# One sink matmul for each pair of heads, and an earlier fetch of the first weight tiles, in a fused attention and MLP kernel

## The chip, the cores and the metric

The kernel runs on one core of a Trainium2 chip. Its engines work side by side, each through a queue of its own, in order: PE (TensorE: matmuls, and transpositions made as matmuls), DVE (VectorE), ACT (ScalarE), POOL (GpSimd) and SP (SyncE, which here only issues DMAs). They wait for one another through semaphores. The metric is the device time of one execution in microseconds, the median of several runs.

## The reference

Attention with sinks and a sliding window, then a two-layer MLP, in float32:

```python
batch, n_heads, seq, head_dim = (4, 8, 768, 64)
n_sink, window = (4, 128)
n_tokens, d_model, d_ff = (3072, 512, 2048)
...
scores = scale * np.matmul(q, k.transpose(0, 1, 3, 2))
is_sink = pos[None, :] < int(n_sink)
in_window = (rel >= 0) & (rel < int(window))
scores = np.where(is_sink | in_window, scores, -1000000000.0)
a = np.exp(scores - np.max(scores, axis=-1, keepdims=True))
a = a / (np.sum(a, axis=-1, keepdims=True) + 1e-09)
x = np.matmul(a, v)        # heads side by side: (3072, 512)
...
h = x @ w_in
out = np.maximum(0.01 * h, h) @ w_out
```

## The kernel before

**Units, heads, steps.** The work is cut into eight units `u`: a batch and one half of its 768 rows, three blocks of 128 rows each (`T = 3`, `TU = 384` columns). A unit has eight heads in four pairs. The attention of a unit is a stream of 60 steps (`attention_stream`), its MLP a stream of 112 steps (`mlp_stream`, 16 slices `fc` of the hidden width). Units 0 and 1 (`u < EARLY`) take the plain path, units 2 to 7 a path with split operands. PE's order is written out by hand: the loop at the end of `fast_path` first draws 70 attention steps alone (`att_steps + LEAD0`), then weaves both streams, about two MLP steps for each attention step, so that the MLP of unit `u` runs beside the attention of the units after it. The other engines' orders are made by a scheduler from the program.

**Split operands.** From unit 2 on, and in the MLP always, a float32 operand is taken as a sum of two parts, hi (rounded by a cast) and lo (the rest, a subtraction), and a product is made of three: hi x hi, hi x lo, lo x hi. For weights the cast is on ScalarE (L179) and the subtraction on GpSimd (L180); for queries and keys L235, L236, L238; for values L249 and L250.

**A head.** Each of three row blocks `j` has its scores (L270, a bank of PSUM of its own, `s`, one buffer), a mask (L298), the row maximum (L306, which frees the bank), the exponential (L309) and the division (L310, L311, L315). `tail` turns a block round on PE (L355), copies hi on ScalarE (L362) and lo on VectorE (L363), and GpSimd places both in `pt` (L324). The sums over the keys of the window are `values` (L411).

**Sinks.** The four sink columns of both heads of a pair are gathered in `sk`, transposed once for the pair (L376), and multiplied with a mask `diag` into `sn` (L380), with 16 or 24 rows: row block, head, sink. From unit 2 on they are split: ScalarE copies hi to rows 0 on of a tile `st` (L386), VectorE subtracts lo into rows 32 on (L387, `SKL = 32`). `values` of a head is a group of six or eight matmuls over hi and lo of `pt` and one more of `st` against the sinks' values `ssp` (L409), 256 or 384 columns wide. A head's matmuls give two products in two halves of a bank `v` (one buffer): ScalarE copies one half (L422), VectorE adds the other (L423), into half of the pair's tile `xf`. `emit_x` then casts it (L483) and subtracts (L484), which gives the MLP's operand.

**Banks for transpositions.** `slot()` hands out the banks for transpositions by a running number `n`. In phase 0 they alternate with the MLP's bank `h`, in phase 1 (the MLP of unit 0) there is one bank `t`, and in phase 2 (from the MLP of unit 1 on) odd numbers have a bank `d` and even ones `t`.

**The MLP.** A slice has twelve matmuls into `h` (L530, one buffer), then ScalarE scales (L537), VectorE takes the maximum (L538, which frees `h`), ScalarE casts (L539) and VectorE subtracts (L540, on GpSimd in unit 0). Nine matmuls (L551) into three banks `o` follow a slice later.

**Weights.** There are 32 tiles of 512 KB. `load_weights` fetches one over SP, decodes it in three VectorE instructions (L171, L173, L175), and splits it. The first four (input and output tile of slices 0 and 1) are called for in the 70 attention steps, at steps 20, 32, 44 and 56. `pace` (L166) holds a fetch until an instruction is done: the decode of the tile four before it (`DEPTH`), or, where there are not four yet, the newest softmax maximum, `anchor[0]`. In units 2 to 5 the MLP's stream also fetches each tile again to check the weights' range (`check_weights`: L191 on ScalarE, L193 on GpSimd, L195 on VectorE).

Of the kernel before, what the change touches and what calls it, by code (L numbers as in the profile page):

```python
# [9 lines left out]
F32 = mybir.dt.float32  # L10
F32R = mybir.dt.float32r
# [3 lines left out]
ALU = mybir.AluOpType  # L15
# [5 lines left out]
P = 128  # L21
B, H, S, D = 4, 8, 768, 64
# [16 lines left out]
NVB = (3, 4)  # L39
# [73 lines left out]
def fast_path(ctx, tc, cpool, qk, vu, vs, w_in, w_out, out, ident, wz, lim, masks, tri, diag, negm, wmin, wmax):  # L113
    nc = tc.nc
# [32 lines left out]
    anchor = [None]  # L147
# [5 lines left out]
        return nc.sync.dma_start(out=raw.rearrange("p f t -> p (f t)"), in_=w_out[fc * P:(fc + 1) * P, :])  # L153

    decoded = []

    def pace(dma, after):
        tc.add_manual_dep(dma.ins, after.ins.name,
                          mybir.DependencyInfo(mybir.DependencyClass.Sync, mybir.DependencyReason.SCHED_ONLY),
                          reason="pace")  # L160

    def load_weights():
        fc, nm = len(wts) // 2, "io"[len(wts) % 2]
        raw = wpool.tile([P, 512, 2], I32, tag=f"w{nm}{fc}", name=f"w{nm}raw{fc}")
        dma = fetch(raw, nm, fc)
        pace(dma, decoded[-DEPTH] if len(decoded) >= DEPTH else anchor[0])  # L166
        top, low = raw[:, :, 1], raw[:, :, 0]
        word = ps_t.tile([P, 512], I32, tag="d", name=f"d{nm}{fc}")
        w = iopool.tile([P, 512], F32, tag="io", name=f"w{nm}f{fc}")
        with tc.issue_after(anchor[0].ins):  # L170
            nc.vector.tensor_scalar(out=word, in0=top, scalar1=3, scalar2=0x3FFFFFFF,  # L171
                                    op0=ALU.logical_shift_left, op1=ALU.bitwise_and)
        nc.vector.scalar_tensor_tensor(out=word, in0=top, scalar=-0x40000000, in1=word,  # L173
                                       op0=ALU.bitwise_and, op1=ALU.bitwise_or)
        decoded.append(nc.vector.scalar_tensor_tensor(out=w.bitcast(I32), in0=low, scalar=29, in1=word,  # L175
                                                      op0=ALU.logical_shift_right, op1=ALU.bitwise_or))
        both = wpool.tile([P, 2, 512], F32R, tag=f"w{nm}{fc}", name=f"w{nm}{fc}")
        hi, lo = both[:, 0, :], both[:, 1, :]
        nc.scalar.copy(out=hi, in_=w)  # L179
        nc.gpsimd.tensor_tensor(out=lo, in0=w, in1=hi.bitcast(F32), op=ALU.subtract)  # L180
        wts[nm, fc] = (hi, lo)
# [60 lines left out]
    def split_values(u, h):  # L242
        vr, sr = vraws.pop((u, h))
        vsp = apool.tile([P, 4, 2 * P], F32R, tag="vsp", name=f"vsp{u}_{h}", bufs=1)
        ssp = apool.tile([SKR, 1, 2 * P], F32R, tag="ssp", name=f"ssp{u}_{h}", bufs=1)
        for dst, src, m in ((vsp, vr, NVB[u % 2]), (ssp, sr, 1)):
            sview = src[:, 0:m * P].rearrange("p (n q c) -> p n q c", q=2, c=D)
            hview = dst.rearrange("p n (q c) -> p n q c", c=D)[:, 0:m, 0::3, :]
            nc.scalar.copy(out=hview, in_=sview)  # L249
            nc.gpsimd.tensor_tensor(out=dst[:, 0:m, D:3 * D].rearrange("p n (q c) -> p n q c", c=D),  # L250
                                    in0=sview, in1=hview.bitcast(F32), op=ALU.subtract)
        return vsp, ssp

    raws = {}
# [116 lines left out]
    def sinks(u, pair, sk):  # L371
        half = u % 2
        nj = T - 1 + half
        rows = nj * 2 * NSK
        tp = slot()
        nc.tensor.transpose(out=tp[0:rows, 0:P], in_=sk[:, 0:nj].rearrange("p j h s -> p (j h s)"),  # L376
                            identity=ident)
        sn = xpool.tile([SROWS, T, P], F32, tag="xf", name=f"sn{u}_{pair}")
        sv = sn[0:rows, 0:nj, :]
        nc.vector.tensor_tensor(out=sv, in0=tp[0:rows, 0:P].rearrange("p (o q) -> p o q", o=1).broadcast_to([rows, nj, P]),  # L380
                                in1=diag[0:rows, 0:nj, :], op=ALU.mult)
        sv = sv.rearrange("p j q -> p (j q)")
        if u < EARLY:
            return sv
        st = sts[half]
        nc.scalar.copy(out=st[0:rows, :], in_=sv)  # L386
        nc.vector.tensor_tensor(out=st[SKL:SKL + rows, :], in0=sv, in1=st[0:rows, :].bitcast(F32),  # L387
                                op=ALU.subtract)
        return st

    def values(u, h, pt, st, state):
        half = u % 2
        pair, odd = divmod(h, 2)
        q0 = 0 if half else P
        hp = slice(odd * D, (odd + 1) * D)
        lp = slice((1 - odd) * D, (2 - odd) * D)
        vv, sv = state["v"]
        if u < EARLY:
            if not odd:
                state["acc"] = ps_v.tile([P, 512], F32, tag="v", name=f"v{u}_{h}")  # L400
            out = state["acc"][hp, :]
            mms = [(vv[:, kb * P + odd * D:kb * P + (odd + 1) * D], pt[:, 0, po:po + m], qo, m)
                   for kb, (po, qo, m) in enumerate(segments(half))]
        else:
            out = ps_v.tile([P, 512], F32, tag="v", name=f"v{u}_{h}")
            cs = slice(odd * P, (odd + 1) * P)
            mms = [(vv[:, kb, cs], pt[:, c, po:po + m], qo, m)
                   for kb, (po, qo, m) in enumerate(segments(half)) for c in range(2)]
            mms.append((sv[:, 0, cs], st, q0, TU - q0))  # L409
        for c, (l, r, o, m) in enumerate(mms):  # L410
            nc.tensor.matmul(out[:, o:o + m], lhsT=l, rhs=r, start=c == 0, stop=c == len(mms) - 1,  # L411
                             skip_group_check=True)
        if u < EARLY:
            if odd:
                nc.tensor.matmul(state["acc"][:, q0:TU], lhsT=sv[0:st.shape[0], :], rhs=st, start=False, stop=True,  # L415
                                 skip_group_check=True)
            x = state["acc"][:, 0:TU]
        else:
            if not odd:
                state["xf"] = xpool.tile([P, TU], F32, tag="xf", name=f"xf{u}_{pair}")  # L420
            x = state["xf"]
            nc.scalar.copy(out=x[hp, :], in_=out[lp, 0:TU])  # L422
            nc.vector.tensor_tensor(out=x[hp, :], in0=out[hp, 0:TU], in1=x[hp, :], op=ALU.add)  # L423
        if odd:
            emit_x(u, pair, x)

# [326 lines left out]
def layout(q, k, v, n_sink, window, moe_w_in, moe_w_out):  # L753
    import numpy as np
    c = np.ascontiguousarray
# [13 lines left out]
    s4 = v[:, :, 0:NSK].reshape(B, NPAIR, 2, NSK, D)  # L769
    for r in range(0, SROWS, 2 * NSK):  # L770
        for x in range(2):
            vs[:, :, 0:2, r + x * NSK:r + (x + 1) * NSK, x] = s4[:, :, None, x]
    vs = vs.reshape(B, NPAIR, SKR, P)
    return [("qk0", c(qk0)), ("qk1", c(qk1)), ("vu0", c(vu0)), ("vu1", c(vu1)), ("vs", c(vs)),
            ("qT", c(qt)), ("kT", c(kt)), ("v", c(v)), ("lims", np.stack([n_sink, window])),
# [17 lines left out]
```

## Time and profile before

| | |
|---|---|
| median of 3 runs | 731.52 us (731.45 to 731.6) |
| the profiled execution | 733.14 us |
| its span (first to last instruction) | 731.3 us |
| mean granted clock of PE | 0.993 |
| sink matmuls of units 2 to 7 (L411, `st` and `ssp`) | 48: 24 of 256 columns, 24 of 384 |
| L386 on ScalarE, L387 on VectorE | 24 each, median 460 and 482 ns |
| DMA | 77.77 MB, mean 106 GB/s |
| first MLP matmul | 51.05 us from the span's start |
| first MLP matmul of unit 1 | 149.56 us |

A row of the timeline gives the start, the length, the engine, the source line, the operation, the tile written and the tiles read, the shape, how many in a row, and in square brackets the idle time before it and what ended it. PE's matmuls overlap, so that the distance from one start to the next says more of a matmul's price than its recorded length. Unless said otherwise, times are from the span's start.

### The profile page before, as it was taken

Reading aid. Unit: us, or ns where it says so; the run is one execution under the profiler, and the core shown is the slowest. Engines: PE = TensorE matmul, PEld = TensorE weight load, DVE = VectorE, ACT = ScalarE, POOL = GpSimd, SP = SyncE. Lnnn points to the kernel's source line nnn. Section 1 sums busy time; section 2 is a strip of 40 time slices with the busy share of each in tenths; the row PEclk is TensorE's granted clock in tenths of the full one; section 3 lists DMA queues with packets and bytes.
Section 4 is the critical chain, followed back from the end, with each engine's and each line's share of the span. In section 5 each row is a group of like instructions: output and inputs, shape, how many; then the busy total and the mean of one; then the engine's idle time right before and its main releaser. Section 6 shows DMA issues by size and latency. Waiting matters only on the chain.

```text
span 731.3 us, 12474 instructions
## 1 busy us (share of the span) xinstructions
PE 709.2 (97%) x3871; PEld 619.9 (85%) x3871; DVE 547.3 (75%) x1749; ACT 422.2 (58%) x1178; POOL 370.5 (51%) x500
## 2 busy tenths in 40 slices
PE   8889999999999999999999999999999999999996
PEld 5457887888999889999988989999888999899995
DVE  6778988666667888888888898888888977733222
ACT  5566766667666666656666566666656565522221
POOL 2115657745456677747566676756666555300000
PEclk9999999999999999999999999999999999999999
DMA  5767766221222533234334333324342211001001
GB/s 174 242 211 216 222 193 218 67 95 38 63 70 69 174 116 108 73 130 145 96 98 127 131 106 112 117 88 148 106 127 81 96 62 41 0 1 44 1 0 49
DMA packets 43755, 77.77 MB, mean 106 GB/s; under 512 B 3616, under 2 KB 26400, under 8 KB 43680
## 3 DMA queue, kind: packets, MB, share of 16 engines
q1 hardware_dynamic: 43536, 76.76, 33.1%
q8 instruction: 33, 0.54, 0.3%
q14 instruction: 42, 0.34, 0.1%
q10 hardware_dynamic: 144, 0.13, 0.1%
HBM read 70.58 MB, written 6.29 MB: 105 GB/s over the span
## 4 chain that ended last, share of the span: by engine, by line
PE 83%; DVE 8%; DMA 4%; ACT 3%; issue 1%; SPq 0%; ACTq 0%; DVEq 0%
PE h L530 33%; PE o L551 33%; PE v L411 8%; PE s L270 6%; PE t L355 2%; DVE gl L540 1%; DMA wiraw<-in_w_in 1%; PE warm L575 1%; DMA woraw<-in_w_out 1%; DVE zeroi L195 1%; DVE g L538 1%; DMA coraw<-in_w_out 1%; DMA vsraw<-in_vs 1%; PE v L415 1%; PE t L342 1%
## 5 line engine op out<-in xcount | busy, mean ns | idle before, releaser
L530 PE MATMUL h<-xh,wi 128*128 128x384 f32 x1024 | 314.5, 354 | 1.3 <-DVE g L538 1.3
L551 PE MATMUL o<-wo,gh 128*128 128x512 f32 x768 | 244.4, 399 | 0.0
L530 PEld LDWEIGHTS h<-xh,wi 128*128 128x128 f32 x1024 | 190.5, 188 | 14.2 <-DVE g L538 2.4
L530 PE MATMUL h<-xl,wi 128*128 128x384 f32 x512 | 172.6, 337 | 0.0
L551 PE MATMUL o<-wo,gl 128*128 128x512 f32 x384 | 151.4, 394 | 0.0
L551 PEld LDWEIGHTS o<-wo,gh 128*128 128x128 f32 x768 | 133.8, 188 | 18.1 <-issue 1.8
L324 POOL TENSOR_SCALAR_AFFINE_SELECT pt<-stg 128x256 fp32r<-128x256 f32 x240 | 100.9, 446 | 84.6 <-DVE stg L363 72.0
L538 DVE TENSOR_TENSOR g<-h,g 128x384 f32<-128x384 f32 x128 | 71.0, 555 | 64.0 <-ACT g L537 62.3
L540 DVE TENSOR_TENSOR gl<-g,gh 128x384 fp32r<-128x384 f32 x112 | 92.1, 823 | 16.6 <-ACT gh L539 15.0
L537 ACT ACTIVATE g<-h 128x384 f32<-128x384 f32 x128 | 62.2, 486 | 71.8 <-PE h L530 71.7
L530 PEld LDWEIGHTS h<-xl,wi 128*128 128x128 f32 x512 | 97.0, 189 | 3.3
L236 POOL TENSOR_TENSOR qksp<-qkraw,qksp 64x392 fp32r<-64x392 f32 (+1 forms) x48 | 58.4, 1217 | 62.2 <-issue 45.1
L309 ACT ACTIVATE pk<-pk,negm 128x128 f32<-128x128 f32 (+1 forms) x144 | 58.0, 403 | 50.3 <-DVE negm L306 49.3
L551 PEld LDWEIGHTS o<-wo,gl 128*128 128x128 f32 x384 | 72.2, 188 | 16.9 <-DVE gl L540 0.3
L539 ACT CAST gh<-g 128x384 fp32r<-128x384 f32 x128 | 65.7, 513 | 33.3 <-DVE g L538 30.7
L270 PEld LDWEIGHTS s<-qksp 128*128 128x128 f32 x288 | 53.1, 188 | 7.8 <-issue 1.7
L270 PE MATMUL s<-qksp 128*128 128x260 f32 (+1 forms) x288 | 56.4, 277 | 1.1 <-DVE negm L306 1.1
L238 POOL TENSOR_TENSOR qksp<-qkraw,qksp 128x384 fp32r<-128x384 f32 x48 | 53.9, 1124 | 3.7
L362 ACT CAST stg<-t 128x128 fp32r<-128x128 f32 x120 | 30.8, 257 | 41.6 <-PE t L355 34.7
L411 PEld LDWEIGHTS v<-pt,vsp 128*128 128x128 f32 x336 | 45.1, 189 | 5.8 <-issue 3.3
L315 DVE TENSOR_SCALAR pk<-pk,sm 128x132 f32<-128x132 f32 (+1 forms) x120 | 47.0, 392 | 2.3
L235 ACT CAST qksp<-qkraw 128x776 fp32r<-128x776 f32 (+1 forms) x48 | 42.8, 892 | 8.6 <-PE s L270 8.4
(131 smaller groups left out, 1079.1 us busy)
## 6 DMA issues: line engine op xcount, KB each, us to landing
qkraw<-in_qk SPq DMA_DIRECT2D x27, 454.0 KB, 3.2
qkraw<-in_qk SPq DMA_DIRECT2D x26, 388.0 KB, 3.1
wiraw<-in_w_in SPq DMA_DIRECT2D x16, 512.0 KB, 3.7
woraw<-in_w_out SPq DMA_DIRECT2D x16, 512.0 KB, 4.4
ciraw<-in_w_in SPq DMA_DIRECT2D x16, 512.0 KB, 3.8
coraw<-in_w_out SPq DMA_DIRECT2D x16, 512.0 KB, 3.6
out<-ob SPq DMA_DIRECT2D x23, 256.0 KB, 2.0
vraw<-in_vu SPq DMA_DIRECT2D x14, 256.0 KB, 2.6
```

Source lines behind the costliest of these rows:

```text
L236: nc.gpsimd.tensor_tensor(out=sp[D:P, TU:TU + n], in0=raw[D:P, TU:TU + n], in1=sp[D:P, TU:TU + n].bitcast(F32), op=ALU.subtract)
L238: nc.gpsimd.tensor_tensor(out=sp[:, TU + n:2 * TU + n], in0=raw[:, 0:TU], in1=sp[:, 0:TU].bitcast(F32), op=ALU.subtract)
L270: nc.tensor.matmul(ps[:, 0:kn], lhsT=sp[:, off + j * P:off + (j + 1) * P], rhs=sp[:, TU + k0:TU + k0 + kn], start=c == 0, stop=c == len(pa ...
L309: nc.scalar.activation(out=w, in_=w, func=AF.Exp, scale=-1.0, bias=neg, accum_out=sm)
L324: nc.gpsimd.affine_select(out=out, in_=src, pattern=([[0, x]] if x > 1 else []) + [[sign, P]], base=-1 if prev else 0, channel_multiplier= ...
L411: nc.tensor.matmul(out[:, o:o + m], lhsT=l, rhs=r, start=c == 0, stop=c == len(mms) - 1, skip_group_check=True)
L530: nc.tensor.matmul(ph[:, 0:TU], lhsT=w[:, cs], rhs=x, start=cc == 0 and c == 0, stop=cc == NCC - 1 and c == 2)
L537: nc.scalar.mul(g, ph[:, 0:TU], 0.01)
L538: anchor[0] = nc.vector.tensor_tensor(out=g, in0=ph[:, 0:TU], in1=g, op=ALU.max)
L539: nc.scalar.copy(out=gh, in_=g)
L540: (nc.gpsimd if u == 0 else nc.vector).tensor_tensor(out=gl, in0=g, in1=gh.bitcast(F32), op=ALU.subtract)
L551: nc.tensor.matmul(po[t], lhsT=gg[:, tsl], rhs=w, start=f == 0 and c == 0, stop=f == NFC - 1 and c == 2)
```

## The change

There are two edits.

**Sinks.** The values of the sinks now come from the host in three groups of 32 rows where there were two. `split_values` makes one tile `ssp` of 128 columns: values hi in the first group, lo in the second, hi in the third. `sinks` fills three groups of `st` to match: hi, hi (a second ScalarE cast), lo (the subtraction, now on GpSimd). One matmul for the pair gives all three products for both heads, since the rows of the other head hold zeros in the value columns. It goes into a bank from `slot()`, ahead of the odd head's group, and VectorE adds it to `xf` after the odd head's L423.

**Weights.** `anchors` keeps the anchor of every step of the 70; the first four tiles wait for the one of twelve steps ago (`PRED = 12`) in place of the newest.

```diff
-        pace(dma, decoded[-DEPTH] if len(decoded) >= DEPTH else anchor[0])
+        pace(dma, decoded[-DEPTH] if len(decoded) >= DEPTH else anchors[-PRED])
...
-        ssp = apool.tile([SKR, 1, 2 * P], F32R, tag="ssp", name=f"ssp{u}_{h}", bufs=1)
-        for dst, src, m in ((vsp, vr, NVB[u % 2]), (ssp, sr, 1)):
...
+        ssp = apool.tile([SKR, P], F32R, tag="ssp", name=f"ssp{u}_{h}", bufs=1)
...
+        nc.scalar.copy(out=ssp, in_=sr)
+        nc.gpsimd.tensor_tensor(out=ssp[SKL:2 * SKL, :], in0=sr[SKL:2 * SKL, :],
+                                in1=ssp[SKL:2 * SKL, :].bitcast(F32), op=ALU.subtract)
...
         nc.scalar.copy(out=st[0:rows, :], in_=sv)
-        nc.vector.tensor_tensor(out=st[SKL:SKL + rows, :], in0=sv, in1=st[0:rows, :].bitcast(F32),
+        nc.scalar.copy(out=st[SKL:SKL + rows, :], in_=sv)
+        nc.gpsimd.tensor_tensor(out=st[2 * SKL:2 * SKL + rows, :], in0=sv, in1=st[0:rows, :].bitcast(F32),
                                 op=ALU.subtract)
...
+            if odd:
+                acc = slot()
+                nc.tensor.matmul(acc[:, q0:TU], lhsT=sv, rhs=st, start=True, stop=True)
...
-            mms.append((sv[:, 0, cs], st, q0, TU - q0))
...
             nc.vector.tensor_tensor(out=x[hp, :], in0=out[hp, 0:TU], in1=x[hp, :], op=ALU.add)
+            if odd:
+                nc.vector.tensor_tensor(out=x[:, q0:], in0=acc[:, q0:TU], in1=x[:, q0:], op=ALU.add)
...
         next(stream)
+        anchors.append(anchor[0])
...
-            vs[:, :, 0:2, r + x * NSK:r + (x + 1) * NSK, x] = s4[:, :, None, x]
+            vs[:, :, 0:3, r + x * NSK:r + (x + 1) * NSK, x] = s4[:, :, None, x]
```

The edits also move instructions on other engines. Line numbers after the change are higher by 1 from `load_weights` on, by 4 from the softmax on, by 7 at L423 and by 9 in `mlp_stream`.

SP's queue in the first part of the run, before (`wiraw0` is the fetch of the input tile of slice 0, `woraw0` of the output tile, `wiraw2` of the input tile of slice 2; `qkraw` and `qkn` are queries and keys, `vraw` and `vn` values):

```order
L205 DMA qkn0_4_254<-in_qk0 128x776
L205 DMA qkraw0_5_296<-in_qk0 128x776
L218 DMA vraw0_4_334<-in_vu0 128x384
L218 DMA vsraw0_4_335<-in_vs 128x128
L152 DMA wiraw0_317<-in_w_in 128x4x256
L205 DMA qkn0_6_353<-in_qk0 128x776
L205 DMA qkn0_7_405<-in_qk0 128x776
L153 DMA woraw0_395<-in_w_out 128x1024
L218 DMA vn0_6_433<-in_vu0 128x384
L218 DMA vsraw0_6_434<-in_vs 128x128
L152 DMA wiraw2_660<-in_w_in 128x4x256
L205 DMA qkraw1_0_452<-in_qk1 128x908
```

After:

```order
L206 DMA qkn0_4_254<-in_qk0 128x776
L152 DMA wiraw0_317<-in_w_in 128x4x256
L206 DMA qkraw0_5_296<-in_qk0 128x776
L219 DMA vraw0_4_334<-in_vu0 128x384
L219 DMA vsraw0_4_335<-in_vs 128x128
L153 DMA woraw0_395<-in_w_out 128x1024
L206 DMA qkn0_6_353<-in_qk0 128x776
L152 DMA wiraw2_660<-in_w_in 128x4x256
L206 DMA qkn0_7_405<-in_qk0 128x776
L219 DMA vn0_6_433<-in_vu0 128x384
L152 DMA wiraw1_476<-in_w_in 128x4x256
L219 DMA vsraw0_6_434<-in_vs 128x128
```

The weight fetches stand earlier, the first one ahead of the load of head 5.

VectorE over the same stretch, before, where the decode of the first tile (`di0`, `wif0`) comes among the softmaxes of head 4 of unit 0 (`pe0_4`):

```order
L282 ISA pe0_4_355,negm_65<-s0_4_0_358,m0_86 128x128
L282 ISA negm_65 128x1
L287 TENSOR_SCALAR sm0_3_299<-sm0_3_299 128x3
L288 RECIPROCAL sm0_3_299<-sm0_3_299 128x3
L294 TENSOR_SCALAR pe0_3_298<-pe0_3_298,sm0_3_299 128x128
L294 TENSOR_SCALAR pe0_3_298<-pe0_3_298,sm0_3_299 128x260 x2
L282 ISA pe0_4_355,negm_65<-s0_4_1_366,wide0_143 128x260
L282 ISA negm_65 128x1
L171 TENSOR_SCALAR di0_319<-wiraw0_317 128x512
```

After:

```order
L172 TENSOR_SCALAR di0_319<-wiraw0_317 128x512
L493 TENSOR_TENSOR xl0_0_310<-v0_0_263,xh0_0_309 128x384
L286 ISA pe0_3_298,negm_65<-s0_3_2_338,wide1_151 128x260
L286 ISA negm_65 128x1
L174 SCALAR_TENSOR_TENSOR di0_319<-wiraw0_317,di0_319 128x512
L286 ISA pe0_4_355,negm_65<-s0_4_0_358,m0_86 128x128
L286 ISA negm_65 128x1
L291 TENSOR_SCALAR sm0_3_299<-sm0_3_299 128x3
L176 SCALAR_TENSOR_TENSOR wif0_320<-wiraw0_317,di0_319 128x512
L292 RECIPROCAL sm0_3_299<-sm0_3_299 128x3
L286 ISA pe0_4_355,negm_65<-s0_4_1_366,wide0_143 128x260
```

The whole decode now stands ahead of the division of head 3 (L294 before, L298 after), about one head earlier than before.

VectorE in the first pair of unit 3, around the odd head (`s3_3` are the scores of head 3, `g2_2` the MLP's slice 2 of unit 2, `zeroi0` the first weight check), before:

```order
L306 ISA pk3_3_3087,negm_65<-s3_3_0_3089,m2_88 128x132
L306 ISA negm_65 128x1
L538 TENSOR_TENSOR g2_2_3102<-h2_2_3054,g2_2_3102 128x384
L310 TENSOR_SCALAR sm3_3_0_3093<-sm3_3_0_3093 128x1
L311 RECIPROCAL sm3_3_0_3093<-sm3_3_0_3093 128x1
L195 ISA zeroi0_3050,wmin_66<-magi0_3049,zeroi0_3050 128x512
L195 ISA wmin_66 128x1
L315 TENSOR_SCALAR pk3_3_3087<-pk3_3_3087,sm3_3_0_3093 128x132
L423 TENSOR_TENSOR xf3_0_3041<-v3_1_3109,xf3_0_3041 64x384
L540 TENSOR_TENSOR gl2_2_3104<-g2_2_3102,gh2_2_3103 128x384
L298 COPY_PREDICATED s3_3_1_3131<-tri_89,s3_3_1_3131 128x128
L306 ISA pk3_3_3087,negm_65<-s3_3_1_3131,m2_88 128x132
```

After:

```order
L196 ISA zeroi0_3058,wmin_66<-magi0_3057,zeroi0_3058 128x512
L196 ISA wmin_66 128x1
L547 TENSOR_TENSOR g2_2_3110<-h2_2_3062,g2_2_3110 128x384
L314 TENSOR_SCALAR sm3_3_0_3101<-sm3_3_0_3101 128x1
L315 RECIPROCAL sm3_3_0_3101<-sm3_3_0_3101 128x1
L319 TENSOR_SCALAR pk3_3_3095<-pk3_3_3095,sm3_3_0_3101 128x132
L430 TENSOR_TENSOR xf3_0_3049<-v3_1_3119,xf3_0_3049 64x384
L549 TENSOR_TENSOR gl2_2_3112<-g2_2_3110,gh2_2_3111 128x384
L302 COPY_PREDICATED s3_3_1_3141<-tri_89,s3_3_1_3141 128x128
L432 TENSOR_TENSOR xf3_0_3049<-t97_3117,xf3_0_3049 128x384
L310 ISA pk3_3_3095,negm_65<-s3_3_1_3141,m2_88 128x132
L310 ISA negm_65 128x1
```

The addition (L432) stands between the mask and the maximum of the odd head's second block, the subtraction L484 has moved behind that maximum, and the check (L195 before, L196 after) has moved ahead of the MLP's maximum (L538, now L547).

More of the change, by code (lines that the diff above doesn't have):

```diff
@@ L155, in fast_path @@
     decoded = []
+    anchors = []
     def pace(dma, after):
@@ L244, in split_values @@
         vsp = apool.tile([P, 4, 2 * P], F32R, tag="vsp", name=f"vsp{u}_{h}", bufs=1)
-        ssp = apool.tile([SKR, 1, 2 * P], F32R, tag="ssp", name=f"ssp{u}_{h}", bufs=1)
-        for dst, src, m in ((vsp, vr, NVB[u % 2]), (ssp, sr, 1)):
[L247 to L251, printed above, removed]
+        ssp = apool.tile([SKR, P], F32R, tag="ssp", name=f"ssp{u}_{h}", bufs=1)
+        m = NVB[u % 2]
+        sview = vr[:, 0:m * P].rearrange("p (n q c) -> p n q c", q=2, c=D)
+        hview = vsp.rearrange("p n (q c) -> p n q c", c=D)[:, 0:m, 0::3, :]
+        nc.scalar.copy(out=hview, in_=sview)
+        nc.gpsimd.tensor_tensor(out=vsp[:, 0:m, D:3 * D].rearrange("p n (q c) -> p n q c", c=D),
+                                in0=sview, in1=hview.bitcast(F32), op=ALU.subtract)
+        nc.scalar.copy(out=ssp, in_=sr)
+        nc.gpsimd.tensor_tensor(out=ssp[SKL:2 * SKL, :], in0=sr[SKL:2 * SKL, :],
+                                in1=ssp[SKL:2 * SKL, :].bitcast(F32), op=ALU.subtract)
         return vsp, ssp
```

## The prediction

> **What bounds the kernel now.** I read the page's busy shares first and then the windows (columns: the stretch and its length, busy time of PE, PEld, DVE, ACT and POOL, granted TensorE clock, DMA share, GB/s), because a share over the whole span hides stages with different limits.
>
> ```profile
> PE 709.2 (97%) x3871; PEld 619.9 (85%) x3871; DVE 547.3 (75%) x1749; ACT 422.2 (58%) x1178; POOL 370.5 (51%) x500
> ...
> 20.00:40.00 20.00, 16.66 (x75) 10.18 (x74) 15.60 (x56) 11.89 (x39) 3.28 (x6) 0.91 0.80 258
> 40.00:60.00 20.00, 15.71 (x72) 10.69 (x71) 14.66 (x39) 12.83 (x37) 6.81 (x8) 0.91 0.61 193
> 60.00:80.00 20.00, 20.00 (x103) 16.27 (x101) 17.70 (x39) 13.08 (x35) 11.15 (x11) 1.00 0.73 228
> 520.00:620.00 100.00, 99.81 (x567) 90.28 (x567) 83.77 (x289) 60.26 (x172) 60.13 (x84) 1.00 0.28 86
> ```
>
> There are two stages. From 60 us on PE is the bound: a matmul that goes there is worth its own time on PE, as long as no wait grows. From 20 to 60 us PE stands idle for 7.6 us (40 less 16.66 and 15.71) and no engine is full, so a chain of dependences sets the time. The chain of waits over the first 62 us (start, length, what), and below it VectorE's timeline (start, length, operation, idle time before it and who ended it), show how the weights enter that chain:
>
> ```profile
> 17.85 3.82 DMA wiraw<-in_w_in
> 32.31 4.50 DMA wiraw<-in_w_in
> 39.65 4.92 DMA woraw<-in_w_out
> ...
> 21.69 0.69 DVE L171 TENSOR_SCALAR di<-wiraw 128x512 int32<-128x512 int32 x1 [0.77 <-DMA wiraw<-in_w_in]
> 36.84 0.69 DVE L171 TENSOR_SCALAR di<-wiraw 128x512 int32<-128x512 int32 x1 [0.69 <-DMA wiraw<-in_w_in]
> 44.60 0.69 DVE L171 TENSOR_SCALAR do<-woraw 128x512 int32<-128x512 int32 x1 [1.66 <-DMA woraw<-in_w_out]
> ```
>
> Each of these fetches starts only when a softmax of about the same moment is done, and a decode then stands at the head of VectorE's queue until the tile lands, with softmaxes of the attention behind it.
>
> **The change, part by part. (a) The sink matmul.** 24 pairs (six units of four) lose one matmul each, 12 of 256 columns and 12 of 384. Its price is not its recorded duration, since matmuls overlap; I take the distance between starts. A group of seven in a unit with 256 sink columns, a group of nine in one with 384:
>
> ```profile
> 180.38 0.82 PE L411 MATMUL v<-pt,vsp 128*128 128x256 f32 x6
> 181.21 0.63 PE L551 MATMUL o<-wo,gh 128*128 128x512 f32 x2
> ...
> 286.47 1.04 PE L411 MATMUL v<-pt,vsp 128*128 128x128 f32 x8
> 287.57 0.63 PE L551 MATMUL o<-wo,gh 128*128 128x512 f32 x2
> ```
>
> Seven take 0.83 us, or 0.118 each, though some have 128 columns and some 256; nine take 1.10, so that eight at 0.118 leave 0.16 for the one of 384. I take 0.12 and 0.17: 12 x 0.12 + 12 x 0.17 = **3.5 us** less. If only the common 0.118 goes each time it is 2.8; if every one is worth 0.17 it is 4.1.
>
> The removed work comes back elsewhere: a second cast on ScalarE at L386's side, the subtraction on GpSimd in place of L387, and an addition on VectorE behind L423. The addition replaces L387 on VectorE and costs about what L423 costs. Whether it is hidden is decided behind the odd head. The rows of pair 6 (unit 3), PE first:
>
> ```profile
> 290.70 1.09 PE L411 MATMUL v<-pt,vsp 128*128 128x128 f32 x8
> 294.70 0.27 PE L355 MATMUL t<-ident,pk 128*128 128x128 f32 x1
> 295.86 0.40 PE L270 MATMUL s<-qksp 128*128 128x260 f32 x2
> 297.33 0.27 PE L355 MATMUL t<-ident,pk 128*128 128x128 f32 x1
> ...
> 293.18 0.56 DVE L423 TENSOR_TENSOR xf<-v,xf 64x384 f32<-64x384 f32 x1 [0.56 <-ACT xf L422]
> 293.77 0.56 DVE L540 TENSOR_TENSOR gl<-g,gh 128x384 fp32r<-128x384 f32 x1
> 294.37 0.30 DVE L298 COPY_PREDICATED s<-tri,s 128x128 f32<-128x128 int8 x1
> 294.57 0.55 DVE L484 TENSOR_TENSOR xl<-xf,xh 128x384 fp32r<-128x384 f32 x1
> 295.04 0.29 DVE L306 CUSTOM_DVE_ANT_0 pk<-s,m 128x132 f32<-128x132 f32 x1
> ```
>
> The order after puts the addition where L484 stands, and L484 behind L306. So L306, which frees the single bank of the scores, still ends near 295.3, 0.53 us ahead of the scores at 295.86: no wait. The sum's own bank is held until the addition ends at about 295.1, after the transposition at 294.70. Had both the same bank, PE would wait there; but from the second MLP unit on `slot()` alternates between two banks (in the order of unit 3's first pair t97 is the sum and t98 the next transposition), and the next but one comes at 297.33, over 2 us after the addition. Cost: nothing.
>
> PE gets one new wait: the sum's matmul waits for GpSimd's product, with the odd group and all later work of PE queued behind it. GpSimd has room for it near 285 us, and the second cast is as long as L386 (shortest, median, longest in ns):
>
> ```profile
> 286.41 1.03 POOL L236 TENSOR_TENSOR qksp<-qkraw,qksp 64x392 fp32r<-64x392 f32 x1 [1.66 <-issue]
> L386 ACT CAST st<-sn x24: 403/460/515, 157.8 to 639.5; 16x256 fp32r<-16x256 f32 x12, 24x384 fp32r<-24x384 f32 x12
> ...
> PE s L270 <- DVE negm L306: 1.1, 1, 1.1
> PE v L411 <- DVE xf L423: 0.7, 2, 0.4
> PE h L530 <- DVE g L538: 0.3, 1, 0.3
> ```
>
> A subtraction of 384 columns takes about as long as L236's of 392, 1.03 us, and fits into the 1.66 us of idle time ahead of it; the group starts at 290.70, over 3 us later. The second cast, 0.46 us, stands ahead of ScalarE's L537 and delays L538 by up to as much. The last rows are PE's waits from 150 to 640 us (total, times, longest): for L538 it waited once, 0.3 us, in six units. Cost: nothing; without that distance, up to 24 x 0.46 = 11 us.
>
> **(b) The early fetch.** Only the first four tiles change their release; later ones wait for a decode, as before. The release moves twelve steps back, which is also the distance between two of them, and the old releases show what that is (SP's row for the second tile below): the second tile's new release is the first one's old one, 17.85 us against 22.75, and the fourth's is the third's, 32.31 against 39.65. All four land before their decode, so the three waits of the rows above go: 0.77 + 0.69 + 1.66 = **3.1 us**, all on the chain. On SP the first tile moves ahead of one score load and the third MLP tile (i2) ahead of another; no engine waits for a score load now. What is late next: the decode itself, which now stands one head earlier among the softmaxes (three instructions of 0.69 us, 2.1 us a tile). If two of the four tiles hold up a softmax by all of that, and nothing else shortens, 3.1 us saved turn into 1.1 lost. On the other side stand two stretches at half clock, one of them this (the release named above, a window, two pieces of the chain, PE's longest wait of the first 60 us, and the MLP's first matmul):
>
> ```profile
> 22.75 0.33 SPq L153 DMA_DIRECT2D woraw<-in_w_out  x1
> ...
> 29.00:30.00 1.00, 1.00 (x3) 0.46 (x2) 0.94 (x5) 0.64 (x4) 0.00 (x0) 0.50 0.86 246
> ...
> 14.82 1.23 PE v L411 x6
> 28.34 2.33 PE v L411 x6
> ...
> PE t L346 <- DVE pe L294: 5.8, 4, 2.4
> ...
> 51.05 0.72 PE L530 MATMUL h<-xh,wi 128*128 128x384 f32 x1
> ```
>
> The same six matmuls take 2.33 us there and 1.23 at full clock, 1.1 more; with the scores and transpositions beside them I estimate 1.6 us for a stretch, 3.2 for both. If the shorter waits avoid them, (b) is worth 6.3. I take 3.1, the sum of the waits that rows show.
>
> The Trainium skill, "TensorE: Matmul & The Clock Gate", Part 1, says that the clock falls to half when a window of about 3.4 us was idle. The longest wait of PE here is 2.4 us, so by the letter of it there would be no half clock to save; the trace shows one all the same, so less idle time than a whole window is enough here. By the rule the sum stays 3.1; by the trace it may reach 6.3.
>
> **(c) The odd head's wait.** In the waits from 150 to 640 us above, the row of v is a group waiting for its bank. The sum's matmul, which uses another bank, now stands ahead and covers 0.12 to 0.17 us each time, and L387 no longer delays L423: **0.3 us** less, between 0 and 0.7.
>
> **(d) The weight check.** In 12 pairs VectorE's new order puts the check L195 ahead of the maximum L538 that frees the MLP's bank. In most its input is long there. In the first pair of unit 3 it is not:
>
> ```profile
> 246.97 1.51 POOL L193 TENSOR_SCALAR zeroi<-magi 128x512 f32<-128x512 f32 x1 [0.78 <-ACT magi L191]
> 248.51 1.77 DVE L195 CUSTOM_DVE_ANT_0 zeroi<-magi,zeroi 128x512 f32<-128x512 f32 x1 [0.40 <-POOL zeroi L193]
> 249.70 0.34 PE L530 MATMUL h<-xh,wi 128*128 128x384 f32 x1
> ```
>
> L538 would follow L195, at 250.2, and end near 250.8: PE, due at 249.7, waits 1.1 us; the 1.1 us wait for L306 just behind it may stay or shrink. I take **1.0 us** more, between 0 and 2.1.
>
> **Sum.** The profiled execution took 733.14 us (span 731.3), 1.6 above the median of 731.52. 733.1 - 3.5 - 3.1 - 0.3 + 1.0 = 727.2; less 1.6 it is **725.6 us**. The ends are 4.1 + 6.3 + 0.7 = 11.1 less (720.4) and 1.1 + 2.1 - 2.8 = 0.4 more (731.9).
>
> **Rivals.** *The start gives nothing:* the decodes turn waits for a DMA into waits for a softmax. For it: VectorE is busy for 15.6 of 20 us there. Against it: it stands still for 3.1 us on the fetches alone, and the chain runs through them. 725.6 + 3.1 = 728.7.
>
> *The half clock goes too:* then (b) is 6.3, and the time 722.4. For it: the waits that precede the low clock shorten. Against it: one decode more stands ahead of them.
>
> *Slower, GpSimd holds VectorE:* 24 new subtractions run on GpSimd beside VectorE, and a collision is dear:
>
> ```profile
> 370.04 1.60 POOL L236 TENSOR_TENSOR qksp<-qkraw,qksp 64x524 fp32r<-64x524 f32 x1 [2.03 <-issue]
> 370.40 1.67 DVE L540 TENSOR_TENSOR gl<-g,gh 128x384 fp32r<-128x384 f32 x1
> ```
>
> L540 took 1.67 us beside that subtraction against 0.56 at 293.77, 1.11 more. If GpSimd's work shifts so that L540 behind the odd head is held like this, L306 ends 1.11 us later; it decides from 0.53 us on, where PE's scores begin to wait. 24 x (1.11 - 0.53) = 13.9 more: 739.5. Against it: L387, a subtraction of the same kind, leaves VectorE, and the new one runs near the sinks' transposition, some 8 us ahead of that L540. The Trainium skill, "SBUF — State Buffer", section "SBUF: two separate sides", says that an instruction of VectorE with two SBUF inputs and one of GpSimd exclude each other for a whole instruction; the trace agrees with 1.67 against 0.56.
>
> **How the numbers follow.** Forecast 0.55, no gain at the start 0.23, half clock gone 0.14, slower 0.08. The measurement can tell about 0.2%, 1.5 us, from no change: faster is below 730.1, slower above 733.0. Faster: nearly all of the first three, 0.86; within 0.2%: their upper tails, 0.07; slower 0.07. The range, 721.5 to 729.5, takes in the first three cases, and leaves out the ends that need several bounds at once.
>
> **What would show it.** Right: no wait of VectorE for wiraw or woraw ahead of 50 us, the first h matmul about 3 us ahead of 51.05, 24 sink matmuls where there were 48, PE idle as little as now from 150 to 640 us. Wrong: PE waiting for pe L294 as long as before (start), PE's scores or transpositions waiting for VectorE in every pair (d, or GpSimd), a long wait of h for g at the check.

## The result, and the profile after

The changed kernel takes 727.49 us, the median of nine runs (724.46 to 729.39), beside 733.18 us for the kernel before on the same chip (nine runs too, 731.45 to 733.77 but for one of 1790.31). The ratio is 0.9917 (95% interval 0.9903 to 0.9931): faster by 0.83%, where 0.81% was forecast. The profiled execution took 727.55 us, span 725.8 us.

So the total was nearly as forecast. The parts were not: the early fetch, priced at 3.1 us, gave nothing; the odd heads' waits gave 2.4 us where 0.3 was expected; and the weight check, priced at 1.0 us, cost nothing. These errors cancel (3.1 too much; 2.1 and 1.0 too little), so that the total came out near is luck. Line numbers of the changed kernel stand a few higher: the decode L171 is L172, the row maximum L306 is L310, the check L195 is L196, the values L411 are L418, L423 is L430, the MLP's L530, L538, L540, L551 are L539, L547, L549, L560. The sum's matmul is L412, its addition L432.

The page's busy shares and the windows (columns as before):

```profile
PE 704.9 (97%) x3847; PEld 617.5 (85%) x3847; DVE 537.9 (74%) x1749; ACT 429.2 (59%) x1202; POOL 393.4 (54%) x524
...
20.00:40.00 20.00, 15.46 (x72) 9.73 (x70) 15.96 (x56) 12.06 (x42) 4.52 (x7) 0.91 0.79 266
40.00:60.00 20.00, 16.66 (x75) 11.30 (x75) 13.32 (x40) 13.00 (x37) 4.75 (x7) 0.92 0.52 147
60.00:80.00 20.00, 20.00 (x103) 16.46 (x102) 17.70 (x40) 12.76 (x33) 11.45 (x11) 1.00 0.76 240
520.00:620.00 100.00, 100.00 (x569) 90.66 (x568) 83.77 (x288) 61.84 (x176) 62.84 (x88) 1.00 0.25 77
```

PE has 24 matmuls fewer and is now busy for all of 520 to 620 us. From 20 to 60 us it still stands idle, for 7.9 us where it was 7.6. The timeline shows the first instruction of each early decode, and the MLP's first matmul:

```profile
17.98 0.69 DVE L172 TENSOR_SCALAR di<-wiraw 128x512 int32<-128x512 int32 x1
24.49 0.69 DVE L172 TENSOR_SCALAR do<-woraw 128x512 int32<-128x512 int32 x1
31.45 0.70 DVE L172 TENSOR_SCALAR di<-wiraw 128x512 int32<-128x512 int32 x1
40.88 0.69 DVE L172 TENSOR_SCALAR do<-woraw 128x512 int32<-128x512 int32 x1
...
52.19 0.53 PE L539 MATMUL h<-xh,wi 128*128 128x384 f32 x1
```

No row has a wait in brackets: all four tiles were there. Yet the MLP starts at 52.19 us, 1.1 us later than the 51.05 of before. The whole gain of the span lies behind it: from the first MLP matmul of unit 1 to the last matmul it was 574.8 us (149.56 to 724.36) and is 568.6 us (150.16 to 718.77), 6.2 us less. This stretch is called **the late part** below, and the first MLP matmul **the start**. Stretches of half clock, 3.41 us each, move the start: 6.8 us of them lie ahead of it here, 5.7 in the profile of before. The mean clock differs from one execution of a kernel to the next, so starts are compared where as much half clock lies ahead of them.

Where the 6.2 us went comes from the distances between the starts of PE's matmuls, added up over the late part: the values and sums with the L551 that follow them (the first L551 behind a group takes longer after the change, so the two are counted together) fell from 283.8 to 280.3 us, the MLP's first product and the transpositions with the waits behind them from 258.2 to 255.4 (252.22 + 5.98; 249.84 + 5.53). That is 3.5 us of matmuls and 2.8 us of waits; the scores took 0.1 us more.

### The profile page after: what moved, and what is told of

Read it like the earlier page. It is cut to its first block, busy times and chain, and to the rows that moved or that the text cites. A ratio compares the mean times of both kernels' runs of the same rounds, so it can differ in the third digit from the quotient of the medians.

```text
span 725.8 us, 12514 instructions
## 1 busy us (share of the span) xinstructions
PE 704.9 (97%) x3847; PEld 617.5 (85%) x3847; DVE 537.9 (74%) x1749; ACT 429.2 (59%) x1202; POOL 393.4 (54%) x524
## 4 chain that ended last, share of the span: by engine, by line
PE 93%; DVE 3%; ACT 1%; DMA 1%; issue 1%; POOL 0%; SPq 0%; DVEq 0%; ACTq 0%
PE h L539 36%; PE o L560 36%; PE v L418 8%; PE s L274 7%; PE t L359 2%; PE warm L584 1%; DVE pe L286 1%; PE v L422 1%; PE t L346 1%; DVE pe L298 1%; DMA vsraw<-in_vs 1%; DMA ciraw<-in_w_in 1%; PE t L380 1%; PE t L347 0%; PE t L412 0%
## 5 line engine op out<-in xcount | busy, mean ns | idle before, releaser
L539 PE MATMUL h<-xh,wi 128*128 128x384 f32 x1024 | 314.2, 353 | 1.0 <-DVE g L547 1.0
L560 PE MATMUL o<-wo,gh 128*128 128x512 f32 x768 | 247.0, 403 | 0.0
L539 PEld LDWEIGHTS h<-xh,wi 128*128 128x128 f32 x1024 | 190.3, 188 | 13.5 <-DVE g L547 1.8
L539 PE MATMUL h<-xl,wi 128*128 128x384 f32 x512 | 172.5, 337 | 0.0
L328 POOL TENSOR_SCALAR_AFFINE_SELECT pt<-stg 128x256 fp32r<-128x256 f32 x240 | 104.5, 460 | 93.8 <-DVE stg L367 72.1
L560 PE MATMUL o<-wo,gl 128*128 128x512 f32 x384 | 151.9, 395 | 0.0
L560 PEld LDWEIGHTS o<-wo,gh 128*128 128x128 f32 x768 | 132.3, 189 | 18.3 <-issue 1.8
L547 DVE TENSOR_TENSOR g<-h,g 128x384 f32<-128x384 f32 x128 | 71.0, 555 | 63.7 <-ACT g L546 62.6
L539 PEld LDWEIGHTS h<-xl,wi 128*128 128x128 f32 x512 | 96.9, 189 | 3.6
L560 PEld LDWEIGHTS o<-wo,gl 128*128 128x128 f32 x384 | 72.1, 188 | 16.9 <-DVE gl L549 0.3
L549 DVE TENSOR_TENSOR gl<-g,gh 128x384 fp32r<-128x384 f32 x112 | 73.4, 655 | 11.6 <-ACT gh L548 9.9
L239 POOL TENSOR_TENSOR qksp<-qkraw,qksp 128x384 fp32r<-128x384 f32 x48 | 52.2, 1087 | 3.8
L302 DVE COPY_PREDICATED s<-tri,s 128x128 f32<-128x128 int8 x120 | 34.7, 289 | 18.0 <-PE s L274 16.7
L418 PEld LDWEIGHTS v<-pt,vsp 128*128 128x128 f32 x336 | 45.1, 189 | 2.4 <-DVE xf L430 0.4
```

The source lines that it names most:

```text
L239: nc.gpsimd.tensor_tensor(out=sp[:, TU + n:2 * TU + n], in0=raw[:, 0:TU], in1=sp[:, 0:TU].bitcast(F32), op=ALU.subtract)
L328: nc.gpsimd.affine_select(out=out, in_=src, pattern=([[0, x]] if x > 1 else []) + [[sign, P]], base=-1 if prev else 0, channel_multiplier= ...
L539: nc.tensor.matmul(ph[:, 0:TU], lhsT=w[:, cs], rhs=x, start=cc == 0 and c == 0, stop=cc == NCC - 1 and c == 2)
L547: anchor[0] = nc.vector.tensor_tensor(out=g, in0=ph[:, 0:TU], in1=g, op=ALU.max)
L549: (nc.gpsimd if u == 0 else nc.vector).tensor_tensor(out=gl, in0=g, in1=gh.bitcast(F32), op=ALU.subtract)
L560: nc.tensor.matmul(po[t], lhsT=gg[:, tsl], rhs=w, start=f == 0 and c == 0, stop=f == NFC - 1 and c == 2)
```

## The experiments

Medians are in us, with the ratio to the kernel before, timed on the same chip. The last two columns are from each one's profile; in brackets is the length of half clock ahead of the start, in us.

| kernel | median | ratio (95%) | start | late part |
|---|---|---|---|---|
| before | 732.54 to 733.18 | | 51.05 (5.7) | 574.8 |
| changed | 727.49 | 0.9917 (0.9903 to 0.9931) | 52.19 (6.8) | 568.6 |
| sinks alone | 727.05 | 0.9927 (0.9909 to 0.9945) | 51.52 (6.8) | 568.3 |
| fetch alone | 733.26 | 1.0003 (0.9989 to 1.0017) | 52.40 (6.8) | 574.3 |
| sum's matmul twice | 733.75 | 1.0008 (0.9995 to 1.0021) | 51.86 (6.8) | 575.1 |
| decode placed late | 727.51 | 0.9936 (0.9913 to 0.9959) | 50.13 (0) | 568.8 |
| lo on VectorE | 727.33 | 0.9936 (0.9920 to 0.9953) | 49.28 (0) | 570.3 |
| sum behind the odd group | 726.55 | 0.9925 (0.9909 to 0.9941) | 49.34 (0) | 569.9 |
| before, lo on GpSimd | 731.91 | 0.9989 (0.9977 to 1.0000) | 49.38 (0) | 573.1 |
| fillers on PE | 731.97 | 0.9990 (0.9976 to 1.0005) | 55.09 (3.4) | 569.0 |
| short decode | 722.75 | 0.9869 (0.9848 to 0.9889) | 46.20 (3.4) | 568.6 |
| transpositions later | 729.29 | 0.9958 (0.9943 to 0.9973) | 51.21 (0) | 569.0 |
| transpositions between | 730.80 | 0.9971 (0.9959 to 0.9983) | 53.13 (6.8) | 569.6 |
| two tiles ahead | 723.39 | 0.9876 (0.9856 to 0.9897) | 47.26 (3.4) | 570.5 |

**Which part gains: sinks alone, fetch alone.** The first has `anchor[0]` in `pace` again; the second is the kernel before with `anchors[-PRED]`.

> The sink edit alone; the release of the first four weight tiles is the old one. Theory A (my reading of the two traces): the whole gain sits in the sinks. From the first MLP matmul of unit 1 on, the trace of after is 6.1 us shorter than that of before (149.56 to 724.36 against 150.16 to 718.77), because besides the 24 matmuls nearly all of PE's waits for the bank v and the scores behind it are gone. Then this kernel takes 6 us less than before, about 727.2 us beside 733.2, and its first MLP matmul stands near 51.05 us as in before. Rival B (the sum on record): the sinks are worth 2.8 us (3.5 + 0.3 - 1.0) and the fetch the rest; then it takes 2.8 us less, 730.4 us. From 4.4 us less on, A is nearer.

> The early release alone; the sinks as in before. Theory A: VectorE's waits for the tiles go, but PE waits for the softmaxes behind the decodes instead, so the first MLP matmul stays between 50.5 and 52.5 us, and the time is that of before but for the stretches at half clock, each worth about 1.7 us, which fall differently from run to run: 731.5 to 735 us, median within 1.2 us of before. Rival B (the sum on record): 3.1 us less than before, about 730.1 us, first MLP matmul near 48 us.

The sinks alone give 6.0 us by the medians, as theory A said, and 5.4 by the ratio (4.0 to 6.7). The fetch alone costs 0.2 us, within an interval of 0.8 less to 1.2 more. The sum on record is refuted in its parts. The waits of 8 to 51 us (total, times, longest) show what the early fetch did. VectorE before, then VectorE and PE with the fetch alone:

```profile
DVE pe L282 <- PE s L270: 5.7, 6, 1.9
...
DVE do L171 <- DMA woraw<-in_w_out: 1.7, 1, 1.7
DVE di L171 <- DMA wiraw<-in_w_in: 1.5, 2, 0.8
```

```profile
DVE pe L283 <- PE s L271: 9.8, 11, 2.9
...
PE t L347 <- DVE pe L295: 6.6, 5, 2.3
```

VectorE waited 5.7 + 1.7 + 1.5 = 8.9 us for scores and tiles, and now waits 9.8 us for scores alone. PE's wait for the normalised block, 5.8 us before, is 6.6 here. The waits changed their name and did not shrink.

**The price of the sum's matmul.**

```diff
                 nc.tensor.matmul(acc[:, q0:TU], lhsT=sv, rhs=st, start=True, stop=True)
+                nc.tensor.matmul(acc[:, q0:TU], lhsT=sv, rhs=st, start=True, stop=True)
```

> The changed kernel with each sum's sink matmul issued twice (24 matmuls more, to the same bank, the second overwrites the first; the result is the same). This prices the matmul by itself. On record a sink matmul is worth 0.12 us at 256 columns and 0.17 at 384: 3.5 us more than the changed kernel, about 731 us. Theory A says the same of the matmul (the rest of the gain came from waits, and they do not come back): +2.8 to +4.1. Rival C: the whole 6 us are the price of 24 matmuls, 0.25 us each: then +6 us, about 733.5. Compared from the first MLP matmul of unit 1 on, where the half clock of the start plays no part.

The late part is 6.5 us longer than the changed kernel's, rival C's number, but not for C's reason. By the distances the 24 matmuls of `acc` took 3.50 us in the changed kernel and 48 take 6.95 here: 3.45 us for 24, as on record. The rest is eight waits of PE's scores for L310: 4.4 us by the distances, where there was one of 1.2. Theory A had the price right and missed that these waits come.

**Why the odd head's waits went.** Three edits: the subtraction of `st` back on VectorE in the changed kernel; the sum's matmul behind the odd group; and the kernel before with only L387 moved.

```diff
-        nc.gpsimd.tensor_tensor(out=st[2 * SKL:2 * SKL + rows, :], in0=sv, ...
+        nc.vector.tensor_tensor(out=st[2 * SKL:2 * SKL + rows, :], in0=sv, ...
```

> The changed kernel with the subtraction that fills the third group of st on VectorE, where the kernel before had its own (L387). It asks why the odd head's waits for the bank v went (seven waits, 2.4 us beyond the usual distance, in the trace of before; none in that of after). Theory E: because a subtraction of 0.48 us left VectorE ahead of the even head's addition, which frees the bank. Then waits of v for xf come back here, 1.0 to 2.4 us in all, and the stretch from the first MLP matmul of unit 1 to the last matmul grows from 568.6 us to between 569.6 and 571; time 728.5 to 730. Rival F: because the sum's matmul stands ahead of the odd group and fills the wait, or because the rest of VectorE's order changed: 568.6 within 0.5, no wait of v, time as the changed kernel, 727.5.

> The changed kernel with the sum's matmul behind the odd head's group instead of ahead of it, so that it covers no wait for the bank v. Theory E (VectorE's queue): the group is due 0.12 or 0.17 us earlier and the bank is free by then in all but two of the 24 pairs (VectorE's addition ends 0.3 us or more before the group starts in 22 of them): at most 0.3 us more, 568.4 to 568.9 from the first MLP matmul of unit 1 on, time 727.5 within 1. Rival F (the cover is what counts): seven waits of about 0.15 us each come back, 1 us or more, 569.6 on.

> The kernel before with one edit: the subtraction L387 on GpSimd instead of VectorE; two sink matmuls a pair as before, nothing added. Theory E: the seven waits of the odd head go, or most of them, and the stretch from the first MLP matmul of unit 1 to the last matmul falls from 574.8 us to 572.4 to 573.4; time 730.8 to 732 beside 733. Rival F: 574.8 within 0.5, waits as before, time 733.

Moving only L387, in the kernel before, saves 1.7 us of the late part (574.8 to 573.1) and 0.8 us of the time by the ratio (0 to 1.7). By the distances, the waits ahead of odd groups fall from 2.4 us in seven places to 1.0 in five: that is theory E, in part. With the subtraction back on VectorE in the changed kernel, no odd group waits. So the sum's matmul ahead of the group, or the order on VectorE that came with it, is enough without that move, and E fails there although its range is met. The 1.7 us of that kernel (568.6 to 570.3) are one wait of the scores, at one pair (lo on VectorE):

```profile
415.62 1.28 POOL L251 TENSOR_TENSOR vsp<-vraw,vsp 128x512 fp32r<-128x512 f32 x1
416.05 1.27 DVE L549 TENSOR_TENSOR gl<-g,gh 128x384 fp32r<-128x384 f32 x1
418.15 0.48 PE L274 MATMUL s<-qksp 128*128 128x260 f32 x2 [1.54 <-DVE negm L310]
```

The kernel with two tiles ahead, at the end of this section, has the same wait at the same pair, and its sinks are those of the changed kernel. It is therefore not a price of this subtraction alone.

With the sum behind the group, two odd groups wait, 0.7 us together: as many as E counted, and not F's seven. The rest of its 1.3 us are waits of the scores for L310, so E's bound of 0.3 fails too. So the move by itself takes over half of the 2.4 us, and the changed kernel without the move all of it. How the sum's matmul ahead of the group does that was not separated: by its own time (0.12 us in four of the seven places, 0.17 in three) it covers about 1.0 us, and the rest must come from the order. Kernels of the table with the changed kernel's sinks have late parts of 568.3 to 570.5 us, so one or two microseconds in one profile are not yet a price. That the two variants do cost something is borne out by the spans of their runs at a mean clock of 0.997 or 0.998: 725.2 to 725.7 us with lo on VectorE and 724.2 to 725.2 with the sum behind, where the changed kernel has 722.7 and 723.0.

**What the start hangs on.** First its decodes' place (the call six steps later, the release by the same softmaxes), then PE's idle time (on the sinks alone, four matmuls of zeros ahead of a head's first transposition):

```diff
-PRE0 = 8
+PRE0 = 14
...
-        pace(dma, decoded[-DEPTH] if len(decoded) >= DEPTH else anchors[-PRED])
+        pace(dma, decoded[-DEPTH] if len(decoded) >= DEPTH else anchors[-PRED - 6])
```

> The changed kernel, with each of the first four weight tiles called for six steps later and released by the anchor of eighteen steps ago: the DMAs are released by the same softmaxes as in the changed kernel, but the decodes stand in VectorE's queue about where they stood in the kernel before. Theory A (the decode that moved ahead among the softmaxes gives back what the fetch saved): no wait of VectorE for the tiles, and the first MLP matmul 2 to 3 us earlier than the 52.19 of the changed kernel, 49 to 50 us, time 724 to 726 us. Rival D (those waits were never on the path, or the start is set by the half clock, whose stretches fall by chance): first MLP matmul 51 to 52.5 us, time as the changed kernel, 727.5 us within 1.5.

```diff
         tp = slot()
+        if j == 0 and phase[0] == 0:
+            for _ in range(4):
+                nc.tensor.matmul(tp[:, 0:TU], lhsT=wz[:, 0:P], rhs=wz, start=True, stop=True)
```

> The sink edit alone (old release), and in the first 70 attention steps four bfloat16 matmuls of zeros of 384 columns ahead of each head's first transposition, into the bank that the transposition then overwrites: they fill the longest waits of PE (t for the normalised row block, up to 2.4 us, 5.5 us in all). Theory G (the spread of the times is the half clock, and it comes from PE's waits in the first 50 us): over the 23 runs of before, 9 of after and 12 of the early release alone a run's span is the longer the lower its mean clock, and at the highest clocks (0.997 and 0.998) it is 728.2 to 728.4 us for the kernels with the old sinks and 722.7 to 723.0 for the new. Then the clock here stays at 0.996 or above in most runs, and the time falls to 724.5 to 726. Rival H: idle time elsewhere sets the half clock, or the fillers delay the chain as much as they save: clock 0.992 to 0.995 and 727 us or more.

The start of 50.13 us is near A's numbers, but no half clock lay ahead of it; two kernels of the table without any, their decodes in the early place, start at 49.28 and 49.34. The time is the changed kernel's. Theory A falls: the place isn't it. The fillers made the start 3.6 us later than with the sinks alone (55.09 against 51.52), with less half clock ahead of it, and a clock of 0.996 or above came in only four of twelve runs: theory G falls, and they delay the chain (rival H).

Three kernels without half clock ahead of the start settle what the release is worth. First the one with the old release, then the two with the new:

```profile
49.38 0.44 PE L530 MATMUL h<-xh,wi 128*128 128x384 f32 x1
```

```profile
49.28 0.53 PE L539 MATMUL h<-xh,wi 128*128 128x384 f32 x1
```

```profile
49.34 0.53 PE L539 MATMUL h<-xh,wi 128*128 128x384 f32 x1
```

Between them lies 0.1 us. So next the decodes' own work (for the first four tiles only the first instruction stays), and PE's order:

```diff
-        nc.vector.scalar_tensor_tensor(out=word, in0=top, scalar=-0x40000000, in1=word,
...
+        if len(wts) < 2 * PRE:
+            decoded.append(first)
+        else:
...
```

> The changed kernel with the decode of the first four weight tiles cut to its first instruction (the other two of each tile are left out for these four, so slices 0 and 1 of the MLP use wrong weights): 8 instructions of about 0.68 us less on VectorE ahead of the MLP's start, 5.4 us. It asks what the start hangs on once no fetch is waited for. Theory I (VectorE's own work, the decodes among the softmaxes): the first MLP matmul at full clock, 49.3 us in the runs so far whatever the release, falls by 2 us or more, and the span at clock 0.997 from 722.7 to 720.7 or less. Rival J (the ring of softmax, normalised block and transposition between VectorE, ScalarE and PE, in PE's written order, into whose gaps the decodes fit): 48.8 to 49.8 us at full clock, time as the changed kernel.

```diff
-POPS = (1, 2, 2), (1, 2, 1)
+POPS = (1, 0, 4), (1, 0, 3)
```

> The changed kernel with another order on PE in units 0 and 1: a head's transpositions all stand behind the third scores of the next head, instead of two behind the second and the rest behind the third (POPS 1,0,4 and 1,0,3 for 1,2,2 and 1,2,1). Theory J (the ring sets the start: PE stands 7 to 8 us ahead of transpositions whose block VectorE has not yet normalised): those waits shrink, the first MLP matmul comes 1 to 3 us earlier at full clock (46 to 48 us), time 724.5 to 726.5. Rival K: PE's waits only move to the values and to the next head's scores, whose softmaxes then come late: first MLP matmul 49 to 52 us or later, time 727 or more.

> As the run before, half of it: one transposition of a head behind the second scores of the next head, the rest behind the third (POPS 1,1,3 and 1,1,2). The first transposition stands where it did, behind the second scores, and still waits for the normalised block. Theory J: less than half of the other run's gain, first MLP matmul 48 to 49.5 us at full clock, time 726 to 727.5. Rival K: as the changed kernel or later, 727 to 729.

Theory I holds. The start comes at 46.20 us although it has a stretch of half clock ahead, over 3 us earlier than 49.3, and the time falls by 4.7 us by the medians, 3.5 by the ratios. PE's wait for the normalised block in 8 to 51 us is down from 6.3 us in the changed kernel to a third (short decode):

```profile
PE t L353 <- DVE pe L301: 2.3, 2, 2.1
```

Theory J fails in both orders; the start gets later, K's way. The last run leaves nothing out. It decodes two tiles ahead of the MLP instead of four (`PRE = 2` becomes `PRE = 1`, with the early release and the new sinks):

> The changed kernel with two weight tiles decoded ahead of the MLP's start instead of four (PRE = 1); nothing is left out, the other two decodes, six instructions or 4.1 us of VectorE, stand behind the first MLP matmul. Theory I (the decodes' own work is what the start pays for: the first MLP matmul came 3 to 4 us earlier without eight of twelve instructions): the first MLP matmul comes about 2 to 3 us earlier, 46.5 to 47.5 us at full clock, and the span at clock 0.997 falls by 1 to 3 us if the MLP of unit 0 can hide them, time 724.5 to 726.5 beside 727.5. Rival L: from 60 to 100 us VectorE is busy for 17.70 and 16.93 of 20 us and PE for all of it, so the decodes are only put off: the first MLP matmul comes earlier, but slices 1 and 2 wait for their weights, the first MLP matmul of unit 1 stays at 147.4 us at full clock, and the time at 727 or more.

It is the fastest kernel that leaves nothing out: 723.39 us (722.30 to 724.35, four runs), ratio 0.9876, about 3 us below the changed kernel by the ratios. The start is at 47.26 us, and unit 1's first MLP matmul at 144.79, below the 147.4 that L speaks of: the MLP of unit 0 hides the decodes. Whether it needs the early release was not tried. Its late part is 1.9 us longer, for a reason that the rows show (a DVE row's bracket is empty where it followed the one before at once):

```profile
412.90 1.28 POOL L251 TENSOR_TENSOR vsp<-vraw,vsp 128x512 fp32r<-128x512 f32 x1
412.96 1.64 DVE L549 TENSOR_TENSOR gl<-g,gh 128x384 fp32r<-128x384 f32 x1
414.52 0.55 DVE L432 TENSOR_TENSOR xf<-t,xf 128x384 f32<-128x384 f32 x1
414.99 0.28 DVE L310 CUSTOM_DVE_ANT_0 pk<-s,m 128x132 f32<-128x132 f32 x1
...
415.43 0.48 PE L274 MATMUL s<-qksp 128*128 128x260 f32 x2 [1.54 <-DVE negm L310]
```

That is the slower rival's mechanism, at one pair, though with another of GpSimd's subtractions: the values' L251 beside L549, which takes 1.64 us; the addition and L310 stand behind it, and PE waits 1.54 us. It decided once here, not 24 times.

## Why the prediction came out, step by step

**(a) The matmuls, 3.5 us: right.** Two groups of the changed kernel's timeline, a unit with 256 sink columns and the odd head of one with 384:

```profile
180.92 0.82 PE L418 MATMUL v<-pt,vsp 128*128 128x256 f32 x6
181.57 0.68 PE L560 MATMUL o<-wo,gh 128*128 128x512 f32 x2
...
289.77 0.33 PE L412 MATMUL t<-st,ssp 128*128 128x384 f32 x1
289.94 1.04 PE L418 MATMUL v<-pt,vsp 128*128 128x128 f32 x8
290.81 0.68 PE L560 MATMUL o<-wo,gh 128*128 128x512 f32 x2
```

The sum's matmul is 0.17 us ahead of its group, the price used. The group of six takes 0.65 us to the next L560, 0.18 less than the seven of before (0.83), but the first L560 behind a group takes about 0.05 longer in exchange (median distance 0.28 to the next, 0.23 before). Over the late part the balance is 3.5 us, and doubling the matmuls gives 3.45 again.

**(b) The early fetch, 3.1 us: this step failed.** "All four land before their decode, so the three waits of the rows above go: 0.77 + 0.69 + 1.66 = 3.1 us, all on the chain." The tiles landed and the waits went; the time did not. The sign that the prediction named for this came too: PE waits 6.3 us for the normalised block, 5.8 before. A chain of waits names what came last at each step, not by how much. PE's scores and VectorE's softmaxes run in a ring here, and where VectorE no longer waits for a tile it waits for PE. The rival "the start gives nothing" was the true case of this part, and "the half clock goes too" was not: 6.8 us of it lie ahead of the start in the profile, 5.7 before. What the start does pay for is the decodes' work: eight instructions less were worth over 3 us of start.

**(c) The odd head's wait, 0.3 us: the mechanism was right in kind, the term too small.** It is 2.4 us, the excess of seven distances (3.6 us in all, against 0.17 each) ahead of odd groups before; after, none is left. Both causes that the prediction named play a part, by the experiments above. The forecast took the total from the list of waits, 0.7 us in two. Two of the places before:

```profile
373.74 0.34 PE L530 MATMUL h<-xh,wi 128*128 128x384 f32 x1
374.14 0.89 PE L411 MATMUL v<-pt,vsp 128*128 128x256 f32 x6
...
437.76 0.34 PE L530 MATMUL h<-xh,wi 128*128 128x384 f32 x1
437.76 0.54 DVE L423 TENSOR_TENSOR xf<-v,xf 64x384 f32<-64x384 f32 x1
438.45 0.41 PE L411 MATMUL v<-pt,vsp 128*128 128x128 f32 x2 [0.35 <-DVE xf L423]
```

The second is listed with 0.35 us, though the starts are 0.69 apart where 0.17 is usual. The first isn't listed at all, and loses 0.23. A matmul of 384 columns is recorded for 0.34 us here and holds the next one back for 0.17, and the wait hides under the rest. PE's waits of 150 to 640 us after:

```profile
PE t L359 <- DVE pt L367: 1.2, 1, 1.2
PE s L274 <- DVE negm L310: 1.0, 1, 1.0
```

**(d) The weight check, 1.0 us more: did not come.** VectorE's order was as said, the length was not. GpSimd beside the check, before:

```profile
248.44 1.29 POOL L250 TENSOR_TENSOR vsp<-vraw,vsp 128x512 fp32r<-128x512 f32 x1
```

The same place after:

```profile
248.07 1.22 POOL L328 TENSOR_SCALAR_AFFINE_SELECT pt<-stg 128x256 fp32r<-128x256 f32 x2
248.15 0.88 DVE L196 CUSTOM_DVE_ANT_0 zeroi<-magi,zeroi 128x512 f32<-128x512 f32 x1 [0.48 <-POOL zeroi L194]
248.95 0.55 DVE L547 TENSOR_TENSOR g<-h,g 128x384 f32<-128x384 f32 x1
249.90 0.34 PE L539 MATMUL h<-xh,wi 128*128 128x384 f32 x1
```

GpSimd's work shifted too: beside the check now runs L328, not the values' subtraction L250, and the check takes 0.88 us instead of 1.77. L547 ends at 249.50, 0.4 us before PE needs it. I had moved VectorE's row and left its old neighbour on GpSimd in place.

**The slower rival** did not come in this kernel. The MLP's subtraction, whose collisions it lives from, got shorter on average (mean 825 to 655 ns). The first row is of before, from 60 to 720 us, the second of after:

```profile
L540 DVE TENSOR_TENSOR gl<-g,gh 128x384 fp32r<-128x384 f32 x111 | 91.6, 825 | 16.0 <-ACT gh L539 14.4
```

```profile
L549 DVE TENSOR_TENSOR gl<-g,gh 128x384 fp32r<-128x384 f32 x112 | 73.4, 655 | 11.6 <-ACT gh L548 9.9
```

Why there are fewer collisions in just this order was not tried by itself. That the margin is thin was shown: the sum's matmul twice, lo on VectorE, the sum behind the odd group and two tiles ahead each brought back waits of the scores behind L310.

## What to carry to other kernels

Before a wait on a chain is counted as a gain, ask what the waiting engine would wait for next: with two engines in a ring a removed wait can come back under another name. Here only less work in the ring shortened it. On an engine whose instructions overlap, price instructions and waits by the distance between starts; the list of waits showed 0.7 us of 2.4. Where an instruction moves, move its neighbours on the other engines too before taking over its old length.

## What the runs showed of the hardware

Half clock comes and goes from execution to execution of one kernel. Much of the spread of the times goes with it: the changed kernel's span was 722.7 us at a mean clock of 0.997 and 727.7 at 0.990. In the profiles it comes in stretches of 3.41 or 6.83 us ahead of the MLP's start; one of the kernel before runs on 1.1 us past that start. In the profile of before, the 3.41 us ahead of its two stretches had PE busy for 1.5 and 2.3 us, so a window in which PE was partly busy was enough. It was no sharp threshold: with lo on VectorE, PE was busy for only 1.6 to 1.7 of 3.41 us in two windows on such a grid, and the clock stayed full. The Trainium skill, "TensorE: Matmul & The Clock Gate", Part 1, gives 3413 ns for the window, running freely; the length agrees with the stretches here, and its "≥1 idle window" is not what these profiles show.
